# x and the gate loaded in sixteen transfers of falling row counts instead of one of 128 rows

## The chip, the core and the metric

One core of a Trainium2 chip runs the kernel. The metric is the device time of one execution in microseconds; the profile comes from one profiled execution of the same program. TensorE (PE), VectorE (DVE), ScalarE (ACT), GpSimd (POOL) and SyncE (SP) each run their own list of instructions and wait for each other through semaphores; transfers are issued by SP and ACT, each into a queue of its own (q1 and q10 in the profile), and carried out by 16 DMA engines that both queues share.

## The reference

Two sequences of one token, D = 448, 16 heads of 256, a key and value cache of 4096 positions, all in float32.

```python
x = A_x                                                   # (2, 1, 448)
g = sigmoid((x * gate_w).sum(-1, keepdims=True))
q = (x @ wq).reshape(B, 1, 16, 256).transpose(0, 2, 1, 3)
scores = einsum("bhqd,bhkd->bhqk", q, k_cache) * 256 ** -0.5
o = einsum("bhqk,bhkd->bhqd", softmax(scores), v_cache)
a = o.transpose(0, 2, 1, 3).reshape(B, 1, 4096) @ wo
b = maximum(x @ w1, 0) @ w2
return g * a + (1 - g) * b
```

## The kernel before

The cache is read as 32 units, one for each pair of head and sequence. A unit is 128 partitions of 16384 numbers, 64 KB a partition and 8192 KB in all, half keys and half values. There are three buffers for them (`slot`), and every large transfer goes through these: first wq into slot 2 (56 KB a partition), units 0 and 1 into slots 0 and 1, then, in the loop `more` (L126 to L131), each further unit as soon as its slot is free (`free0` to `free2`), and at the end w1 with w2 into slot 2, and wo into slot 0. All of these are issued by SP, in this order, so that two large transfers stand in its queue most of the time.

xg holds x of both sequences and the gate's weights: 128 rows (partitions) of 12 numbers, 48 bytes a row. ACT issues its transfer (L121) as its first instruction, at the same time as SP issues that of wq. The semaphore `xg` counts 16 for a finished transfer. Two engines wait for it: DVE, which spreads x over columns (`xr`, L167, and `xu`, L169), and PE, which multiplies x with the gate (L178, into `pw`) when xr and xu are there.

Behind this on PE stands the query projection: two halves of 16 matmuls each (32 rows in the trace) on wq in slot 2, each with a scaled copy on ACT (`wide`, L184), four transposes (L181) and the placing of the queries in `qt`. When PE has done these it frees slot 2 (`free2`):

```python
    pr.raw(pe, lambda e: (e.sem_inc(sem["room"], 1), e.drain().then_inc(free[2], 1)))
    pr.raw(act, lambda e: pick(e, 0, 0), have_q)
```

That release lets SP issue the load of unit 2 (L131), for which SP has waited since it issued units 0 and 1. ACT picks the first query (L249), and the loop over the units starts: PE makes the scores (L242), DVE their maximum (L261), ACT the exponentials (L254), and DVE eight passes over the values (L265), the last of which frees the unit's slot. PE may start the scores of the next unit after the first of these eight passes (`room`).

After the units come the second branch (w1, w2), the combination of the parts of the softmax, the output projection with wo, and the store.

Of the kernel before, what the change touches and what calls it, by code (L numbers as in the profile page):

```python
# [8 lines left out]
P, HP = 128, 64  # L9
# [58 lines left out]
def gated_mix_decode(nc, xg, kv, wq, w12, wo, out):  # L68
# [22 lines left out]
    def sbuf(name, *shape):  # L91
        return nc.alloc_sbuf_tensor(name, [*shape], F32).ap()
# [9 lines left out]
    sem = {n: nc.alloc_semaphore(n) for n in names}  # L102
    land = [sem[f"land{s}"] for s in range(SLOTS)]
    free = [sem[f"free{s}"] for s in range(SLOTS)]
    pr = Program(nc)
    pe, dve, act, pool, sp = ENGINES
# [9 lines left out]
    def load(s, src, signal, lo=0, hi=None):  # L116
        hi = src.shape[1] if hi is None else hi
        return lambda e: e.dma_start(slot[s][:, lo:hi], src[:, lo:hi]).then_inc(signal, 16)  # L118

    xg_sb = sbuf("xg_sb", P, KC, B + 1)  # L120
    pr.raw(act, lambda e: e.dma_start(xg_sb, xg).then_inc(sem["xg"], 16))  # L121
    pr.raw(sp, load(2, wq, land[2]))
    for u in range(2):
        pr.raw(sp, load(u, kv[u], land[u]))
# [37 lines left out]


    xr = sbuf("xr", P, KC, G, B, RB)
    pr.raw(dve, lambda e: e.wait_ge(sem["xg"], 16))
    for g in range(G):
        pr.op(dve, lambda e, g=g: e.tensor_copy(xr[:, :, g], xg_sb[:, :, :B, None].to_broadcast([P, KC, B, RB])))  # L167
    xu = sbuf("xu", P, KC, UB // B, B)
# [15 lines left out]
        return pr.op(act, lambda e: e.activation(out, src, fn, **kw), *after)  # L184


    pr.raw(pe, lambda e: e.wait_ge(sem["xg"], 16))
    for c in range(KC):
        r = rows_of(c)
        t = mm(pw[0][:, :1], xr[r, c].rearrange("p g b r -> p (g b r)"), xg_sb[r, c, B:], c == 0, c == KC - 1, have_x)  # L190
# [264 lines left out]
```

## Time and profile before

| | us |
|---|---|
| median of 3 runs | 676.48 (676.11 to 676.78) |
| profiled execution | 675.89 |
| its span, first to last instruction | 674.6 |
| busy: DVE, PE, ACT | 341.5, 220.4, 59.7 |
| first DVE copy of x starts | 20.78 |
| load of unit 2 issued | 37.18 |

In the profile a row of the timeline gives start, duration, engine, line, what is written from what, and in brackets how long the engine was idle before it and what ended that. SPq and ACTq are the issues of transfers. A row of the windows gives a stretch, its length, the busy time of PE, its weight load, DVE, ACT and POOL, the granted clock, the share of the DMA engines and the rate; in short windows the last two count a packet's whole size where it starts, so a share can be over 1. In the DMA section a transfer's last number is the time from its issue to its landing, in which all semaphore counts have come.

### The profile page before, as it was taken

To read this page: it belongs to the slowest core of one execution; us is meant where nothing else is said; L and a number is where in the kernel's file an instruction comes from. 1 tells how busy PE (TensorE), PEld (TensorE's weight loads), DVE (VectorE), ACT (ScalarE), POOL (GpSimd) and SP (SyncE) were. 2 spreads that over 40 slices of the span, in tenths; PEclk is the share of its full clock that TensorE was granted. 3 is DMA by queue.
4 is the path that set the end of the run, shared out by engine and by line. 5 is a ranking of instruction groups with operands and counts; after the bars stand their busy time and mean duration, and the time that the engine had idled before them with its cause. 6 is when DMAs were issued, how large, how long until landed. Compare 5 with 4: busy or idle time off the path is not lost. (4 is left out here: it accounts for less than half of the span.)

```text
span 674.6 us, 4162 instructions
## 1 busy us (share of the span) xinstructions
PE 220.4 (33%) x1323; PEld 67.6 (10%) x1323; DVE 341.5 (51%) x571; ACT 59.7 (9%) x121; POOL 0.7 (0%) x6
## 2 busy tenths in 40 slices
PE   0653212333332213333321233333223333331367
PEld 0210000001001000100100010010001001000012
DVE  0006565643655665364566636455564643657661
ACT  0010001001000100100010010001001001000010
POOL 0000000000000000000000000000000000000000
PEclk9976566776656677676556667655666766655789
DMA  9999999999999999999999999999999999999997
GB/s 381 428 435 436 436 435 435 435 435 435 435 435 435 435 435 435 435 435 435 431 435 435 435 435 435 435 435 435 435 435 435 431 435 435 435 435 435 403 424 310
DMA packets 6372, 289.61 MB, mean 429 GB/s; under 512 B 864, under 2 KB 1120, under 8 KB 1632
## 3 DMA queue, kind: packets, MB, share of 16 engines
q1 hardware_dynamic: 6224, 289.55, 99.3%
q8 instruction: 3, 0.05, 0.0%
q10 hardware_dynamic: 144, 0.01, 0.0%
q14 instruction: 1, 0.01, 0.0%
HBM read 289.54 MB, written 0.01 MB: 429 GB/s over the span
## 5 line engine op out<-in xcount | busy, mean ns | idle before, releaser
L265 DVE SCALAR_TENSOR_TENSOR slot<-slot,prob 128x1024 f32<-128x1024 f32 x256 | 295.9, 1221 | 65.3 <-DVEq L65 65.3
L242 PE MATMUL ps<-slot,query 128*32 128x512 f32 x1024 | 186.3, 890 | 406.4 <-PEq L65 406.3
L261 DVE TENSOR_REDUCE nm<-ps 128x1024 f32 (+1 forms) x32 | 39.2, 1224 | 228.8 <-DVEq L65 228.8
L242 PEld LDWEIGHTS ps<-slot,query 128*32 128x32 f32 x1024 | 55.7, 156 | 535.5 <-issue 534.9
L254 ACT ACTIVATE prob<-ps,nm 128x1024 f32<-128x1024 f32 x32 | 35.6, 1113 | 367.2 <-ACTq L65 367.1
L254 ACT ACT_TABLE_LOAD x10 | 12.8, 1283 | 178.7 <-ACTq L65 178.7
L265 DVE DVE_READ_ACCUMULATOR slot<-slot,prob (+1 forms) x256 | 21.2, 83 | 0.0
L178 PE MATMUL pw<-slot,xr 128*32 128x512 f32 (+3 forms) x96 | 13.5, 696 | 1.7 <-PEq L65 1.7
L167 DVE COPY xr<-xg_sb 128x128 f32<-128x128 f32 x4 | 0.6, 220 | 18.5 <-DMA xg_sb<-in_xg 18.5
L178 PE MATMUL pw<-xg_sb,xr 128*128 128x1 f32 (+1 forms) x8 | 1.9, 352 | 21.7 <-DVE xu L169 21.7
L178 PE MATMUL acc<-slot,hr 128*32 128x448 f32 x28 | 6.1, 945 | 2.7 <-DMA slot<-in_w 2.7
L249 ACT ACTIVATE query<-qt 128x2 f32 (+1 forms) x32 | 6.2, 193 | 0.0
L254 ACT ACTIVATION_READ_ACCUMULATOR prob<-ps,nm (+1 forms) x32 | 6.2, 193 | 0.0
L178 PE MATMUL acc<-slot,ot 128*32 128x448 f32 x48 | 5.4, 547 | 1.3 <-DMA slot<-in_wo 1.3
L181 PE MATMUL pw<-ident,nm 128*16 128x128 f32 x2 | 0.7, 330 | 12.6 <-DVEq L315 12.6
L178 PEld LDWEIGHTS pw<-slot,xr 128*32 128x32 f32 (+1 forms) x96 | 2.9, 122 | 10.7 <-issue 10.7
L178 PEld LDWEIGHTS pw<-xg_sb,xr 128*128 128x128 f32 (+1 forms) x8 | 1.8, 320 | 21.6 <-DMA xg_sb<-in_xg 21.6
L181 PE MATMUL pw<-ident,wide 128*128 128x128 f32 x11 | 1.9, 288 | 2.4 <-ACT wide L184 2.4
L383 DVE COPY wide<-acc 128x448 f32<-128x448 f32 x1 | 0.6, 625 | 3.9 <-PE acc L178 3.9
L292 DVE TENSOR_REDUCE nb<-pw 16x1 f32<-16x4 f32 x2 | 0.3, 150 | 4.5 <-PE pw L181 4.5
L178 PE MATMUL pw<-slot,ot 128*32 128x112 f32 x64 | 2.3, 265 | 0.3 <-DMA slot<-in_wo 0.2
L309 DVE COPY ot<-pw 128x256 f32<-128x256 f32 x4 | 1.5, 419 | 1.4 <-PE pw L178 1.4
(42 smaller groups left out, 20.3 us busy)
## 6 DMA issues: line engine op xcount, KB each, us to landing
slot<-in_wq SPq DMA_DIRECT2D x1, 7168.0 KB, 19.8
slot<-in_w SPq DMA_DIRECT2D x2, 3136.0 KB, 30.8
slot<-in_wo SPq DMA_DIRECT2D x2, 1792.0 KB, 20.3
slot<-in_wo SPq DMA_DIRECT2D x3, 896.0 KB, 25.6
slot<-in_kv SPq DMA_DIRECT2D x32, 39.0
slot<-in_wo SPq DMA_DIRECT2D x1, 448.0 KB, 27.9
slot<-in_wo SPq DMA_DIRECT2D x2, 224.0 KB, 28.0
xg_sb<-in_xg ACTq DMA_DIRECT2D x1, 6.0 KB, 20.0
```

Of the source, the lines that this page charges most:

```text
L167: pr.op(dve, lambda e, g=g: e.tensor_copy(xr[:, :, g], xg_sb[:, :, :B, None].to_broadcast([P, KC, B, RB])))
L178: return pr.op(pe, lambda e: e.matmul(out, lhs, rhs, start=start, stop=stop), *after)
L181: return pr.op(pe, lambda e: e.transpose(out, src, ident), *after)
L242: m = e.matmul(ps[g * R:(g + 1) * R, c * CW:(c + 1) * CW], query[s][:, t:t + 1].to_broadcast([P, R]), slot[s][:, lo:lo + CW], start=(t == ...
L249: e.activation(query[s], qt[:, :, bass.ds(u, 1)].rearrange("p t o -> p (t o)"), AF.Copy).then_inc(sem["query"], 1)
L254: e.activation(prob, ps, AF.Exp, bias=nm[:, bass.ds(u, 1)], accum_out=ls[:, bass.ds(u, 1)]).then_inc(sem["prob"], 1)
L261: e.tensor_reduce(nm[:, bass.ds(u, 1)], ps, axis=AX.X, op=ALU.max, negate=True).then_inc(sem["top"], 1)
L265: m = e.scalar_tensor_tensor(v, v, 1.0, prob, op0=ALU.mult, op1=ALU.mult, accum_out=ov[:, bass.ds(u, 1), j])
L292: t = pr.op(dve, lambda e: e.tensor_reduce(nb, mt, axis=AX.X, op=ALU.min), t)
L309: t = pr.op(dve, lambda e, hh=hh: e.tensor_copy(ot[:, i, hh], po[:, hh * B * J:(hh + 1) * B * J].rearrange("p (b j o) -> p j b o", j=J, o= ...
L383: t = pr.op(dve, lambda e: e.tensor_copy(a_sb, acc), t)
```

## The change

The one transfer of 128 rows becomes sixteen, of 15, 14, 13 and so on to 1 rows, and one of 8, issued by ACT one after the other. Each adds 16 to the same semaphore; DVE and PE wait for 256 instead of 16. Bytes, addresses and the rest of the program are the same.

```diff
     xg_sb = sbuf("xg_sb", P, KC, B + 1)
-    pr.raw(act, lambda e: e.dma_start(xg_sb, xg).then_inc(sem["xg"], 16))
+    XG = (*range(15, 0, -1), 8)
+    assert sum(XG) == P
+
+    def load_x(e):
+        lo = 0
+        for k in XG:
+            e.dma_start(xg_sb[lo:lo + k], xg[lo:lo + k]).then_inc(sem["xg"], 16)
+            lo += k
+
+    pr.raw(act, load_x)
...
-    pr.raw(dve, lambda e: e.wait_ge(sem["xg"], 16))
+    pr.raw(dve, lambda e: e.wait_ge(sem["xg"], 16 * len(XG)))
...
-    pr.raw(pe, lambda e: e.wait_ge(sem["xg"], 16))
+    pr.raw(pe, lambda e: e.wait_ge(sem["xg"], 16 * len(XG)))
```

On ACT, at the very start of the program, one issue of 128 rows of 12 numbers stood ahead of the table load and of the gate's activations, which wait for PE:

```order
L60 UNCONDITIONAL_BRANCH [waits barrier_Pool_Activation_PE_DVE_SP_release]
L121 DMA xg_sb<-in_xg 128x12
L184 ACT_TABLE_LOAD
L184 ACTIVATE gp<-pw 128x1 [waits tensor]
L184 ACTIVATE gu<-pw 16x1 [waits tensor]
```

In the changed kernel sixteen stand there (the middle ten are left out here):

```order
L60 UNCONDITIONAL_BRANCH [waits barrier_Pool_Activation_PE_DVE_SP_release]
L128 DMA xg_sb<-in_xg 15x12
L128 DMA xg_sb<-in_xg 14x12
L128 DMA xg_sb<-in_xg 13x12
...
L128 DMA xg_sb<-in_xg 2x12
L128 DMA xg_sb<-in_xg 1x12
L128 DMA xg_sb<-in_xg 8x12
L194 ACT_TABLE_LOAD
L194 ACTIVATE gp<-pw 128x1 [waits tensor]
```

The table load and the first activations of ACT have moved behind fifteen more issues. Nothing moves on the other engines. On SP, the list at the same place shows what the transfers of xg share the DMA engines with, and on which release each load of a unit waits:

```order
L118 DMA slot<-in_wq 128x14336
L118 DMA slot<-in_kv 128x16384 x2
L46 UNCONDITIONAL_BRANCH
L141 ISA [waits free2]
L141 DMA slot<-in_kv 128x16384
L141 ISA [waits free0]
L141 DMA slot<-in_kv 128x16384
```

These rows stand as before, with only the line numbers changed: wq and two units are issued without a wait, unit 2 waits for slot 2, and unit 3 for slot 0.

## The prediction

> **What bounds the kernel now.** I read the shares and the DMA section of the page first, then the start of the timeline, then narrow windows for the DMA engines.
>
> ```profile
> PE 220.4 (33%) x1323; PEld 67.6 (10%) x1323; DVE 341.5 (51%) x571; ACT 59.7 (9%) x121; POOL 0.7 (0%) x6
> DMA  9999999999999999999999999999999999999997
> GB/s 381 428 435 436 436 435 435 435 435 435 435 435 435 435 435 435 435 435 435 431 435 435 435 435 435 435 435 435 435 435 435 431 435 435 435 435 435 403 424 310
> DMA packets 6372, 289.61 MB, mean 429 GB/s; under 512 B 864, under 2 KB 1120, under 8 KB 1632
> q1 hardware_dynamic: 6224, 289.55, 99.3%
> q10 hardware_dynamic: 144, 0.01, 0.0%
> slot<-in_wq SPq DMA_DIRECT2D x1, 7168.0 KB, 19.8
> xg_sb<-in_xg ACTq DMA_DIRECT2D x1, 6.0 KB, 20.0
> out<-res SPq DMA_DIRECT2D x1, 7.0 KB, 1.7
> DMA to landing us min/median/max: 37.0/39.0/57.5
> ```
>
> No compute engine is busy for much over half of the span, while the DMA engines stream at 435 GB/s in nearly every slice. The time is the byte count plus whatever time the stream stands still. So an edit costs only what it adds to the stream, or the time for which it lets the stream run dry. The last row is for the K/V loads: the longest, 57.5 us, is the second one, queued at the start behind wq and the first.
>
> The odd row is xg: 6 KB take 20.0 us to land, as long as the 7168 KB of wq issued at the same moment, while the 7 KB of the output land in 1.7 us once nothing else runs. Hence xg does not travel at its own speed: its pieces wait among wq's.
>
> How big the pieces are: q10 holds 144 packets for xg, which has 128 rows; 16 more are the semaphore writes, one for each of 16 engines. The small packets of the whole program bear this out: 45 transfers times 16 semaphore writes, 128 rows of xg and 16 of the output are 864, the number under 512 B. So each engine has 8 rows of xg and 1 semaphore write, 9 packets, and for wq likewise 8 rows of 56 KB and 1 write. A 56 KB row at 435/16 GB/s takes 2.11 us; a 64 KB row of K/V takes 2.41. The windows show these rows as waves (counted where a packet starts):
>
> ```profile
> 4.60:5.00 0.40, 0.00 (x0) 0.00 (x0) 0.00 (x0) 0.00 (x0) 0.00 (x0) 1.00 4.65 2009
> 5.00:6.60 1.60, 0.00 (x0) 0.00 (x0) 0.00 (x0) 0.00 (x0) 0.00 (x0) 1.00 0.08 36
> 6.60:7.10 0.50, 0.00 (x0) 0.00 (x0) 0.00 (x0) 0.00 (x0) 0.00 (x0) 1.00 3.99 1722
> 57.50:57.80 0.30, 0.00 (x0) 0.00 (x0) 0.30 (x1) 0.00 (x0) 0.00 (x0) 0.50 0.00 0
> 57.80:58.20 0.40, 0.00 (x0) 0.00 (x0) 0.40 (x1) 0.00 (x0) 0.00 (x0) 0.50 2.66 1147
> 58.20:58.60 0.40, 0.00 (x0) 0.00 (x0) 0.40 (x3) 0.00 (x0) 0.00 (x0) 0.50 3.03 1311
> ```
>
> Second rows of wq start at about 4.7, third ones at 6.8. First rows effectively started at 4.7 - 2.11 = 2.6, which is 1.85 after the issue at 0.75. Eight rows of wq end at 2.6 + 16.9 = 19.5, eight of the first K/V at 38.7, eight of the second at 58.0; the wave at 57.8 to 58.6 is the third K/V load following without a gap. If the two queues take turns packet by packet on each engine, xg's 8 rows go between wq's 8 rows and its semaphore write follows wq's: landing just after wq, which is what the rows say (20.0 against 19.8). One xg packet per packet of the big queue is the reading on which all below rests.
>
> Then the work that waits for xg, from the timeline:
>
> ```profile
> 0.75 0.39 ACTq L121 DMA_DIRECT2D xg_sb<-in_xg  x1
> 1.20 0.91 SPq L118 DMA_DIRECT2D slot<-in_kv  x2
> 20.78 0.63 DVE L167 COPY xr<-xg_sb 128x128 f32<-128x128 f32 x4 [18.48 <-DMA xg_sb<-in_xg]
> 21.66 1.92 PE L178 MATMUL pw<-xg_sb,xr 128*128 128x1 f32 x8 [21.66 <-DVE xu L169]
> 23.90 6.34 PE L178 MATMUL pw<-slot,xr 128*32 128x512 f32 x32
> 31.62 3.77 PE L178 MATMUL pw<-slot,xr 128*32 128x512 f32 x32
> 37.17 0.20 ACT L249 ACTIVATE query<-qt 128x2 f32<-128x2 f32 x1
> 37.18 0.35 SPq L131 DMA_DIRECT2D slot<-in_kv  x1
> 40.30 6.56 PE L242 MATMUL ps<-slot,query 128*32 128x512 f32 x32 [3.46 <-PEq L65]
> 59.42 1.22 DVE L265 SCALAR_TENSOR_TENSOR slot<-slot,prob 128x1024 f32<-128x1024 f32 x1
> 59.81 5.35 PE L242 MATMUL ps<-slot,query 128*32 128x512 f32 x32 [12.94 <-PEq L65]
> 60.88 0.34 SPq L131 DMA_DIRECT2D slot<-in_kv  x1
> 79.75 5.62 PE L242 MATMUL ps<-slot,query 128*32 128x512 f32 x32 [14.59 <-PEq L65]
> ```
>
> xg at 20.78 starts the copies of x; both halves of the query projection follow; then PE frees slot 2, and SP issues the third K/V load at 37.18. From xg to that issue: 16.40 us. The queue is full until 58.0, so this issue could come as late as 58.0 - 1.85 = 56.15 and xg as late as 39.75: the cover is 19.0 us.
>
> **The change part by part.** (1) ACT issues 16 transfers instead of 1. At 0.43 us each (SP's first K/V issues take 0.91 for two, with the gap) the last stands at 0.75 + 15 x 0.43 = 7.2 us. ACT's next work, its table load aside, waits for the gate's matmuls, so this costs 0; a dearer issue of 1 us would end at 16 and is covered as well. (2) The bytes are the same; there are up to 112 more semaphore packets. All of xg's 144 packets stay below 0.05% of 16 engines' span in the page, 0.037 us each at most and probably far less: 0.
>
> (3) The pieces no longer divide by 16. Which engines a transfer of 15 rows uses, no row of this profile shows, since every transfer here has 128 or 16 rows. The bounds: dealt out in rotation, each engine gets 8 rows and 8 semaphore writes, 16 turns; dealt from the same first engine each time, one row to an engine, the first engine gets a row and a write of each of the 16 transfers, 32 turns; all rows of an odd transfer on one engine, up to 128 + 16 = 144. What the big queue has for one engine before the third K/V load is 9 + 9 + 9 = 27 packets. The turn that ends the cover is about the 18th, which follows the first K/V load at 38.7 (landing some 0.5 to 1 us later); each further turn costs 2.41 us; from the 27th on it saturates, since the rest of xg goes through an empty queue. So of the interval from 16 to 144 only 16 to 18 is harmless, and all from 27 on comes to the same. I take 32: the split in all 45 transfers is the same for the same shape, which is what a rule by shape alone gives, and a rotation would need a memory of the transfer before.
>
> The Trainium skill has this price: "DMA: Bandwidth & Descriptors", section "Why a DMA increments its semaphore by 16 and not by 1", says that a transfer from such a queue runs on the largest number of engines up to 16 that divides its slowest dimension, and on the lowest-numbered of them; no run here shows it yet. By it the first engine has 32 turns.
>
> (4) xg's last piece then lands just after the second K/V load on that engine. The rows of that load end at 58.0; xg landed 0.5 to 1.3 after its last turn before (19.5 against 20.75, the slowest engine included). So 58.2 to 59.3; I take 58.7. DVE and PE wait there, and everything behind them.
>
> (5) The third K/V load is issued 16.40 later, at 75.1. The projection is the same work on a PE that has idled as before, so I keep its duration. Now the queue is empty. A load into an empty queue: wq's 19.8 us less 16.87 (7168 KB at 435 GB/s) are 2.93 us of start and end; a K/V load of 8192 KB takes 19.28 + 2.93 = 22.2. It lands at 97.3. Before, its scores start at 79.75, and those of the second load 0.6 after its landing (1.66 + 57.5 = 59.2; 59.81): landing at 79.2. Late by 18.1. The bounds: a start as quick as the output's 1.7 in all saves 0.75; xg between 58.2 and 59.3 gives -0.5 to +0.6.
>
> (6) The fourth load needs slot 0, so the first unit's end. Its query is ready 37.37 - 20.78 = 16.6 after xg, at 75.3; scores from 75.6. Before, its scores took 6.56 and from their end (46.86) to the end of its last DVE pass (60.64) 13.8, and SP issued 0.24 later. Scores now: between 3.77 (the second projection half, as many matmuls at a better clock) and 6.56; I take 5.5, as the later units. End 94.9, issue at 95.1 (93.4 to 96.2). To follow without a gap it should be issued by the end of the third load's rows, 75.1 + 1.85 + 19.28 = 96.2, less 1.85: 94.4. Another 0.7 us (0 to 1.8).
>
> (7) After that the slots are ahead again: a backlogged unit takes some 12 us of DVE (rows of the second unit, below, from its reduction to its last pass) against 19.3 of its load, so nothing else is late and nothing is won back, the stream being at its ceiling.
>
> ```profile
> 65.51 1.22 DVE L261 TENSOR_REDUCE nm<-ps 128x1024 f32 x1 [4.87 <-DVEq L65]
> 76.41 1.22 DVE L265 SCALAR_TENSOR_TENSOR slot<-slot,prob 128x1024 f32<-128x1024 f32 x1
> ```
>
> Sum: 18.1 + 0.7 = 18.8 us. The profiled execution took 675.89 (span 674.6), 0.6 below the median of the runs shown; it becomes 694.7, and the median 676.48 becomes 695.3.
>
> **Rivals.** (a) Not slower: the transfers are dealt round the engines, or a row and its semaphore write pass in one turn. Either makes 16 turns on the busiest engine: 9 of wq, 7 rows of the first K/V load, so xg lands at 19.5 + 7 x 2.41 + 1 = 37.4, inside the cover that ends at 39.75, and the time stays 676.5. It decides at 18 turns. Against it: 864 small packets count the semaphore writes as packets of their own; for it, that no row shows the share of an odd transfer.
>
> (b) One engine for all rows of an odd transfer: the 27 turns are used up in the same way and up to 117 packets are left, at most 0.037 each, 4.3 us: 695.3 to 699.6.
>
> (c) The transfers complete one after the other, each at the output's 1.7 us, and do not queue behind big rows: the last at 20.75 + 15 x 1.7 = 46.3, the third K/V issue at 62.7, 6.5 behind 56.15: 683. Against it: the K/V loads issued 0.46 apart follow one another without a gap. The skill's page "DMA: Bandwidth & Descriptors", section "Anatomy of one DMA — SWDGE (gpsimd) path", puts a fixed 2.0 us on each transfer of the other path; taken as serial, that would be an estimate of 687. No run here shows it.
>
> (d) Faster: nothing in the stream gets shorter; only noise.
>
> **How the numbers follow.** My forecast 0.87, (a) 0.06 with its threshold case, (b) 0.04, (c) 0.02, (d) 0.01. The time is that of the likeliest, 695.3. Its own range, from the bounds in (4) to (6), is 693 to 698. The range for 8 in 10 reaches a little lower, to 691, for a quicker start of an empty queue and a better clock together, and up to 699 for most of (b). A difference under 0.2% (1.35 us; the three runs lie within 0.1%) counts as none: faster 0.01, same 0.05, slower 0.94.
>
> **What the profile after would show.** q10 with about 256 packets (128 rows, and 15 + 14 + ... + 1 + 8 = 128 writes); the first copy of x on DVE near 58.7; the third K/V issue near 75.1; a hole in the GB/s row in the fourth and fifth slice (50.6 to 84.3) worth 18 us, and full slices after it. If q10 has its packets but the copy starts near 37, (a) is right; near 46, (c). If the copy starts at 58.7 and the time is not up by 17 to 20, the empty queue's start or the fourth load's wait is mis-sized.

## Result and the profile after

| | before | changed |
|---|---|---|
| median, us | 676.3 (675.94 to 676.78) | 695.9 (695.79 to 695.93) |
| profiled execution, span, us | 675.89, 674.6 | 695.92, 694.6 |
| first DVE copy of x, us | 20.78 | 59.60 |
| load of unit 2 issued, us | 37.18 | 76.03 |

The ratio is 1.0292 (95% interval 1.0280 to 1.0305): 19.6 us slower, where 18.8 had been forecast (695.3). The two profiled executions differ by 20.0 us in their spans, since the one before lay 0.4 us under its median.

The page after, its DMA rows and the two queues:

```profile
DMA  9992599999999999999999999999999999999997
GB/s 387 459 423 121 242 423 457 438 430 423 426 426 460 438 423 426 423 442 453 430 423 426 426 464 434 423 426 423 460 442 423 426 423 453 442 430 426 419 424 315
q1 hardware_dynamic: 6224, 289.55, 96.6%
q10 hardware_dynamic: 256, 0.01, 0.0%
```

The stream has one hole, in the fourth and fifth slice (52 to 87 us); in every other slice the engines are as busy as before, though the rate now swings between 419 and 464 GB/s where it stood at 435. q10 has 256 packets: 128 rows and 128 semaphore writes, which is one write for each engine that a transfer uses, with as many engines as rows.

These rows of the timeline after show the chain that made the hole:

```profile
0.75 6.46 ACTq L128 DMA_DIRECT2D xg_sb<-in_xg  x16
7.24 1.28 ACT L194 ACT_TABLE_LOAD   x1 [7.24 <-issue]
59.60 0.63 DVE L177 COPY xr<-xg_sb 128x128 f32<-128x128 f32 x4 [57.30 <-DMA xg_sb<-in_xg]
60.49 1.92 PE L188 MATMUL pw<-xg_sb,xr 128*128 128x1 f32 x8 [60.49 <-DVE xu L179]
62.73 6.35 PE L188 MATMUL pw<-slot,xr 128*32 128x512 f32 x32
70.47 3.77 PE L188 MATMUL pw<-slot,xr 128*32 128x512 f32 x32
76.03 0.35 SPq L141 DMA_DIRECT2D slot<-in_kv  x1
76.53 3.64 PE L252 MATMUL ps<-slot,query 128*32 128x512 f32 x32 [0.83 <-PEq L65]
94.16 0.34 SPq L141 DMA_DIRECT2D slot<-in_kv  x1
99.66 6.58 PE L252 MATMUL ps<-slot,query 128*32 128x512 f32 x32 [7.05 <-PEq L65]
```

The sixteen issues are over at 7.2 us, yet DVE waits until 59.60. The projection then runs as before, and SP can issue the load of unit 2 at 76.03 only. In windows of the changed kernel (the last two numbers are the DMA share and GB/s) the engines start their last rows of unit 1 just after 55.5 (1049 GB/s over 1 us is 16 rows of 64 KB) and then nothing but a few small packets until that load arrives:

```profile
55.50:56.50 1.00, 0.00 (x0) 0.00 (x0) 0.00 (x0) 0.00 (x0) 0.00 (x0) 1.00 2.42 1049
56.50:57.90 1.40, 0.00 (x0) 0.00 (x0) 0.00 (x0) 0.00 (x0) 0.00 (x0) 1.00 0.00 0
57.90:58.70 0.80, 0.00 (x0) 0.00 (x0) 0.00 (x0) 0.00 (x0) 0.00 (x0) 1.00 0.02 0
58.70:76.90 18.20, 13.98 (x92) 5.22 (x96) 0.89 (x6) 2.25 (x9) 0.00 (x0) 1.00 0.00 0
76.90:78.00 1.10, 1.10 (x16) 0.46 (x12) 0.00 (x0) 0.00 (x0) 0.00 (x0) 1.00 2.78 953
```

Before, the wave at 57.8 to 58.6 followed here without a gap. The row with 0.00 over 18.2 us is nearly the whole loss. The share of 0.02 at 57.9 to 58.7 holds the last xg packets, passing with unit 1's semaphore writes at the end of its load, where the forecast put them.

### The profile page after: what moved, and what is told of

It reads as the page before. It is cut to its first block, busy times and chain, and to the rows that moved or that the text cites. A ratio compares the mean times of both kernels' runs of the same rounds, so it can differ in the third digit from the quotient of the medians.

```text
span 694.6 us, 4177 instructions
## 1 busy us (share of the span) xinstructions
PE 211.6 (30%) x1323; PEld 64.6 (9%) x1323; DVE 341.4 (49%) x571; ACT 59.8 (9%) x121; POOL 0.7 (0%) x6
## 5 line engine op out<-in xcount | busy, mean ns | idle before, releaser
L252 PE MATMUL ps<-slot,query 128*32 128x512 f32 x1024 | 178.5, 856 | 396.5 <-PEq L65 396.4
L252 PEld LDWEIGHTS ps<-slot,query 128*32 128x32 f32 x1024 | 52.9, 150 | 520.7 <-issue 520.2
```

Source lines behind the costliest of these rows:

```text
L252: m = e.matmul(ps[g * R:(g + 1) * R, c * CW:(c + 1) * CW], query[s][:, t:t + 1].to_broadcast([P, R]), slot[s][:, lo:lo + CW], start=(t == ...
```

## Experiments

The theory to be tested: the two queues take turns packet by packet on each engine, a semaphore write is a turn of its own, the engine with the most xg packets decides, and a delay is free while the big queue still has work (the cover). The rivals: what counts is the number of transfers, each at a fixed price; the uneven shares, or the sixteen transfers themselves, are slow; every microsecond of xg's delay costs one.

**Two transfers only.**

```diff
-    XG = (*range(15, 0, -1), 8)
+    XG = (127, 1)
```

> Two transfers only, of 127 rows and of 1. Turns theory (the queues alternate packet by packet on each engine, and the engine with the most xg packets decides): 127 has no divisor up to 16 but 1, so all rows go to one engine, 130 packets against the 27 of the big queue; xg lands after the second unit's load as with sixteen transfers, plus about 100 packets through an empty queue at the 0.013 us seen between two of them, 1.3 us. First DVE copy near 60.5, time about 697 (696 to 700); q10 shows 130 packets. Count theory (each further transfer costs a turn of 2.42 us, whatever its rows): first copy near 23, time 676.3.

Measured: 694.91 us, ratio 1.0273 (1.0256 to 1.0290). The queue of xg on this kernel's page:

```profile
q10 hardware_dynamic: 130, 0.01, 0.0%
```

And its timeline, the copy of x and the issue for unit 2:

```profile
59.47 0.63 DVE L177 COPY xr<-xg_sb 128x128 f32<-128x128 f32 x4 [57.16 <-DMA xg_sb<-in_xg]
75.09 0.35 SPq L141 DMA_DIRECT2D slot<-in_kv  x1
```

Two transfers cost as much as sixteen, so the number of transfers is not the price. The 130 packets are 128 rows and only one semaphore write for each transfer: each ran on one engine. The copy came 1 us earlier than expected, and the time of 694.91 lies just below the expected 696 to 700. The packet records of the trace (start, length, size and queue of every DMA packet) say why: 55 of the rows had passed by 2.6 us, before wq's first row held that engine, and the 50 packets left after unit 1 followed one another in 0.007 us each, so they cost almost nothing.

**Eight transfers of 16 rows.**

```diff
+    XG = (16,) * 8
```

> Eight transfers of 16 rows, one row on each engine from each: 8 rows and 8 semaphore writes an engine. Turns theory with a semaphore write as a turn of its own: 16 turns, after 9 packets of wq and 7 rows of the first unit: first DVE copy near 37 to 38, inside the cover, time 676.3 as before. Turns theory with the write passing together with its row: 8 turns, first copy near 20.8. Both give no change of time; the copy's start tells them apart. q10 256 packets in both.

Measured: 676.23 us, ratio 1.0002 (0.9993 to 1.0012). Page, timeline and windows of this kernel, in this order:

```profile
q10 hardware_dynamic: 256, 0.01, 0.0%
```

```profile
37.23 0.63 DVE L177 COPY xr<-xg_sb 128x128 f32<-128x128 f32 x4 [34.93 <-DMA xg_sb<-in_xg]
52.76 0.35 SPq L141 DMA_DIRECT2D slot<-in_kv  x1
```

```profile
56.40:58.00 1.60, 0.49 (x8) 0.00 (x0) 0.77 (x1) 0.00 (x0) 0.00 (x0) 1.00 0.00 0
58.00:58.70 0.70, 0.00 (x0) 0.00 (x0) 0.45 (x1) 0.05 (x1) 0.00 (x0) 1.00 3.47 1498
```

The same 256 packets in the queue, but 16 on each engine instead of 32 on the first: the copy starts at 37.23, so each semaphore write does take a turn (8 turns would have given 20.8). xg is 16.5 us later than before and it costs nothing: unit 2's rows follow at 58.0 with no gap beyond the wave's own pause (1.6 us here, as between the waves of the kernel before). That is the cover.

**Twenty, twenty-two and eighteen turns.** Transfers of 16 rows give every engine one row and one write, transfers of 8 give them to eight engines alone, so the turns of the busiest engine can be dialled, two for each transfer.

```diff
+    XG = (16,) * 6 + (8,) * 4
...
+    XG = (16,) * 5 + (8,) * 6
...
+    XG = (16,) * 7 + (8,) * 2
```

> Six transfers of 16 rows and four of 8: engines 0 to 7 get 10 rows and 10 writes, 20 turns; the others 12. Turns theory: the last follows the second row of the second unit (43.6 to 44.3), first DVE copy near 44.5 to 45, 4.8 us past the end of the cover at 39.75: third K/V issue near 61.1, time about 681 (680 to 682). Count theory: 20.78 plus nine times 2.42 is 42.6, time 679. If the big queue were not the cover at all but each us of xg's delay cost a us: 676.3 + 24 = 700.

> Five transfers of 16 rows and six of 8: 22 turns on engines 0 to 7. Turns theory: one row and one write more than with 20 turns, so two rows of the second unit later: first DVE copy near 44.40 + 4.83 = 49.2, third K/V issue 64.5 to 65.6, time 685.2 to 686.2. If a semaphore write took no turn of its own: copy near 46.8, time near 683.

> Seven transfers of 16 rows and two of 8: 18 turns on engines 0 to 7, the edge of the cover. Turns theory: the last row follows unit 0's last row and the last write unit 0's semaphore write, near 39.0: first DVE copy near 39.7, third K/V issue 55 to 56.2, time 676.3 to 676.7, no loss to be measured. If the cover were shorter than the 19.0 us worked out, up to 2 us slower.

| turns | first copy | load of unit 2 issued | median, us | ratio (95% interval) |
|---|---|---|---|---|
| 16 | 37.23 | 52.76 | 676.23 | 1.0002 (0.9993 to 1.0012) |
| 18 | 39.85 | 55.28 | 677.33 | 1.0014 (1.0004 to 1.0023) |
| 20 | 44.40 | 59.64 | 680.38 | 1.0063 (1.0046 to 1.0080) |
| 22 | 49.36 | 64.94 | 684.98 | 1.0131 (1.0110 to 1.0152) |

The timelines, of 20, of 22 and of 18 turns in this order:

```profile
44.40 0.63 DVE L177 COPY xr<-xg_sb 128x128 f32<-128x128 f32 x4 [42.09 <-DMA xg_sb<-in_xg]
59.64 0.35 SPq L141 DMA_DIRECT2D slot<-in_kv  x1
```

```profile
49.36 0.63 DVE L177 COPY xr<-xg_sb 128x128 f32<-128x128 f32 x4 [47.06 <-DMA xg_sb<-in_xg]
64.94 0.35 SPq L141 DMA_DIRECT2D slot<-in_kv  x1
```

```profile
39.85 0.63 DVE L177 COPY xr<-xg_sb 128x128 f32<-128x128 f32 x4 [37.55 <-DMA xg_sb<-in_xg]
55.28 0.35 SPq L141 DMA_DIRECT2D slot<-in_kv  x1
```

From 20 to 22 turns the copy moves by 4.96 us, two rows of a unit (4.83), and the time by 4.6. From 16 to 18 it moves by 2.62: of the two added turns one follows unit 0's semaphore write and not a row. The count of transfers does not fit: for the ten transfers of 20 turns it gave a copy at 42.6 and 679 us, against 44.40 and 680.38.

The time starts to rise near where the cover was worked out to end: copies 4.6 and 9.6 us past 39.75 cost 4.1 and 8.8 us. (With 20 turns the load came 1.5 us before the expected 61.1, since the first half of the projection took 5.18 us and not 6.34.) With 18 turns the load is issued at 55.28, before the 56.15 that was the latest harmless moment. The 1.1 us measured are within what was set as no difference, but 677.33 lies above the expected 676.3 to 676.7 and the interval leaves out 1. The packet records show a part of it: unit 2's first rows start without a gap at 58.05 to 58.59, but they take 2.42 to 3.56 us where all of them took 2.42 with 16 turns. That is 0.28 us on average, and this execution's span is 0.4 us longer than before, so the cover seems to end somewhat before the 56.15 that was worked out. The rest of the 1.1 us stays open.

**The same sixteen transfers in the big queue.**

```diff
-    pr.raw(act, load_x)
     pr.raw(sp, load(2, wq, land[2]))
+    pr.raw(sp, load_x)
```

> The sixteen transfers of the changed kernel, but issued by SP in the big queue between wq and unit 0, so there are no turns between two queues on any engine. Turns theory: the small packets follow wq's rows in order and pass at about 0.013 us each, their semaphore writes landing some 0.17 us apart: first DVE copy near 21 to 23, inside the cover; SP's sixteen issues (about 7 us) end at 8.1, before wq's rows do at 19.5: time 676.3 to 677. If sixteen transfers or their uneven shares cost the time by themselves (issue, completion one after the other, the first engine's load): still 690 to 696.

Measured: 676.8 us, ratio 1.0010 (1.0000 to 1.0020). The timeline of this kernel, then its windows:

```profile
1.20 5.92 SPq L128 DMA_DIRECT2D xg_sb<-in_xg  x16
23.19 0.63 DVE L177 COPY xr<-xg_sb 128x128 f32<-128x128 f32 x4 [20.89 <-DMA xg_sb<-in_xg]
39.95 0.35 SPq L141 DMA_DIRECT2D slot<-in_kv  x1
```

```profile
19.00:20.20 1.20, 0.00 (x0) 0.00 (x0) 0.00 (x0) 0.00 (x0) 0.00 (x0) 1.00 2.83 879
21.50:22.60 1.10, 0.00 (x0) 0.00 (x0) 0.00 (x0) 0.00 (x0) 0.00 (x0) 1.00 1.10 477
22.60:23.20 0.60, 0.00 (x0) 0.00 (x0) 0.01 (x1) 0.00 (x0) 0.00 (x0) 1.00 0.00 0
23.20:24.90 1.70, 0.82 (x4) 0.85 (x5) 0.73 (x5) 0.00 (x0) 0.00 (x0) 1.00 1.42 617
```

The transfers, their shares and their 256 semaphore counts are those of the changed kernel; the turns between two queues are gone, and with them the loss. (SP now issues them, so units 0 and 1 are issued at 7.2 instead of 1.2, long before wq's rows end.) The windows show a small rest. All sixteen engines start unit 0 in the window from 19.00, as they should after wq: 879 GB/s over 1.2 us is 16 rows of 64 KB and the 6 KB of xg. Their second rows are due 2.4 us later, but only eight start in the window from 21.50 (477 GB/s over 1.1 us), and the others after 23.2. In the packet records the first rows of those others took 3.5 to 4.5 us instead of 2.42.

**Even shares on eight engines.**

```diff
+    XG = (8,) * 16
```

> Sixteen transfers of 8 rows: engines 0 to 7 get 16 rows and 16 writes, 32 turns, the other eight none. Turns theory: as with the falling row counts, first DVE copy near 59.5, third K/V issue 75 to 76, time 695 to 696. If what cost the time were the one overloaded engine (sharply uneven shares), eight engines sharing would land it earlier: copy well before 59.

Measured: 695.36 us, ratio 1.0289 (1.0272 to 1.0307). In its timeline:

```profile
59.65 0.63 DVE L177 COPY xr<-xg_sb 128x128 f32<-128x128 f32 x4 [57.35 <-DMA xg_sb<-in_xg]
74.85 0.35 SPq L141 DMA_DIRECT2D slot<-in_kv  x1
```

Eight engines with 32 turns land xg when one engine with 32 does. It also shows that transfers of 8 rows start at the same engines each time: with the starts in rotation this kernel would have had 16 turns, and a copy near 37.

**The sixteen transfers alone.**

```diff
+    pr.raw(sp, lambda e: e.wait_ge(sem["xg"], 16 * len(XG)))
     pr.raw(sp, load(2, wq, land[2]))
```

> The sixteen transfers of the changed kernel, with wq and all behind it issued only when xg has landed, so that xg has the engines to itself. Turns theory: xg lands about 1.3 us after its last issue at 6.9, first DVE copy near 8.5, wq issued near 8.5 instead of 0.75, time 676.3 + 7.8 = 684. If the sixteen transfers were slow by themselves (each 1.7 us, one after the other): copy near 28, time near 704.

Measured: 683.07 us, ratio 1.0099 (1.0082 to 1.0116). In its timeline:

```profile
7.72 0.63 DVE L178 COPY xr<-xg_sb 128x128 f32<-128x128 f32 x4 [5.42 <-DMA xg_sb<-in_xg]
7.72 0.39 SPq L118 DMA_DIRECT2D slot<-in_wq  x1
```

With the engines to themselves the sixteen transfers have landed by 7.72, 1.0 us after the end of their last issue (6.70), and 0.8 before the expected 8.5. Had they gone one after the other, it would have been near 28. wq starts 6.97 us later than before, and the time is 6.85 us longer. So the transfers are not slow by themselves. They are held up.

No variant beat the kernel before, and none was expected to: an xg that arrives earlier only lengthens a cover that is already long enough.

## Why the prediction was right, point by point

- **The bound.** Right: bytes over 435 GB/s plus the hole. Of the 20.0 us by which the span grew, 18.2 are one window without traffic.
- **One xg packet per packet of the big queue, semaphore writes included.** Shown, by 16, 20 and 22 turns landing where their turns put them, and by the loss vanishing when both stand in one queue. The packet records of the changed kernel show it directly: 15 rows of xg pass at 4.54 to 5.24 us, their 15 semaphore writes at 6.67 to 7.36, the 14 rows of the next transfer at 8.79 to 9.48, each one row of wq (2.12 us) after the last.
- **Step 3, the split.** As forecast: as many engines as rows, from the same first one. The 256 packets give the first half, sixteen transfers of 8 rows the second, and two transfers of 127 and 1 the case of one engine. The Trainium skill's rule in "DMA: Bandwidth & Descriptors", section "Why a DMA increments its semaphore by 16 and not by 1" (the largest divisor up to 16, on the lowest-numbered engines) agrees with the 256 and the 130 packets; which numbers the engines bear, these rows do not say.
- **Step 3, saturation.** Shown: 32 and 130 turns give copies at 59.60 and 59.47.
- **Step 1, ACT's issues at no cost.** The last ended at 7.2, as said, and the table load moved from 1.17 to 7.24, long before 62, where ACT is next wanted.
- **Step 4, xg's landing, mis-sized by 0.9.** 59.60 for 58.7, just outside its bounds of 58.2 to 59.3. The last packets of xg did pass by 58.55, but ten semaphore writes pass there together and land one after another, from 58.64 to 59.58, so the last took 1.0 us where before one took about 0.5 (19.44 to 19.96).
- **Step 5, the load into an empty queue, mis-sized by 1.0.** The projection took 16.43 again (76.03 less 59.60). The load took 23.2 and not 22.2:

```profile
DMA to landing us min/median/max: 23.2/38.6/57.5
```

  (The row is that of the K/V loads; its least value is the load of unit 2, the only one issued into an empty queue.) One row of that load came late. Narrow windows of the changed kernel show a wave of 64 KB rows, a pause, and a single row:

```profile
82.40:83.10 0.70, 0.00 (x0) 0.00 (x0) 0.00 (x0) 0.70 (x1) 0.00 (x0) 1.00 3.33 1428
83.10:83.70 0.60, 0.00 (x0) 0.00 (x0) 0.00 (x0) 0.59 (x2) 0.00 (x0) 1.00 0.00 0
83.70:84.00 0.30, 0.00 (x0) 0.00 (x0) 0.00 (x0) 0.30 (x1) 0.00 (x0) 1.00 0.60 218
```

```profile
q8 instruction: 3, 0.05, 0.0%
```

  The wave of 1428 GB/s over 0.7 us is 15 rows and 16 KB more. The packet records name these 16 KB: a packet of the queue q8, which the page lists as `instruction` with three packets. It starts at 82.89, where the sixteenth engine's next row was due, and takes 0.96 us; that row starts at 83.84. Fifteen engines' semaphore writes land by 97.92, which is 21.9 us after the issue, and the last one at 99.22. So the forecast's 22.2 was close for a load without this packet. The kernel of twenty turns bears it out: its first q8 packet comes at 85.9, after the load of unit 2, and that load took 21.9. With 22 turns the packet falls into the load (78.8), and the last engine landed 1.2 us behind the others. The kernel before has such a packet as well, at 62.99, but there it left the last engine only 0.4 us behind. What the packet holds is not shown.
- **Step 6, the fourth load, 0.7 too much.** The scores of the first unit took 3.64 and not 5.5, at a granted clock of 1.00 (the window from 76.90); before, they took 6.56 at a mean of 0.55. So its slot was free and the load issued at 94.16, before 94.4 and well before the 95.3 that this bound becomes when unit 2 is issued at 76.03 instead of 75.1. Even the lower bound of 3.77 was a little long. What kept the clock up is not shown.
- **The sum.** 18.1 + 0.9 + 1.0 and nothing for step 6 is 20.0, the span's 674.6 to 694.6. The scores of unit 2 moved by 99.66 - 79.75 = 19.91, so all of it was lost by then and nothing came back, as step 7 said. The three errors, of 1 us or less each, cancelled in part, and that they did is luck.

## What to carry to other kernels

A transfer's size tells little of when it lands if it shares engines with a large stream: count its packets on its busiest engine, semaphore writes included, and take a full row of the stream for each. Make the row count of a transfer a multiple of 16, so that no engine carries more of it than another, and put a small load that others wait for into the same queue at the place where it is wanted, where it pays no turns (676.8 us here instead of 695.9). And find the cover first: a delay of 16.5 us was free, and what went past the 19.0 us of cover cost nearly its full length.

## What the runs showed of the hardware that was not expected

- The first half of the query projection, the same 32 rows, took 5.13 to 6.67 us at a granted clock of 1.00, the second 3.77 each time. The shortest, from the timeline of sixteen transfers of 8 rows, and the longest, from that of the transfers behind wq:

```profile
62.77 5.13 PE L188 MATMUL pw<-slot,xr 128*32 128x512 f32 x32
```

```profile
26.33 6.67 PE L188 MATMUL pw<-slot,xr 128*32 128x512 f32 x32
```

  That is why the kernel of sixteen transfers of 8 issued unit 2's load 15.2 us after its copy, and the changed kernel 16.4 after its own. What sets the spread stays open.
- A run of small packets with semaphore writes is not free for the engine that carries it: behind wq, eight engines started unit 0's second row about 1.6 us after the others (the windows from 21.50 and from 23.20). The small packets themselves pass quickly, a row with its write every 0.013 us in the packet records, which makes 0.2 us for sixteen of them. It is the 64 KB row behind them that grows. Each engine's count can be matched by its times (wq's last row ends, the small packets pass, unit 0 starts): behind up to four rows of xg with their writes it takes 2.42 us, behind nine 3.53, and behind sixteen 4.45. That kernel's 0.5 us (ratio 1.0010) would fit, but it was not measured by itself.
- The queue that the page lists as `q8 instruction` brings three packets of 16 KB in a run. The one in the load of unit 2 takes a turn of 0.96 us on one data engine, and the load lands later for it: by 1.3 us in the changed kernel, and by 1.4 with sixteen transfers of 8 rows (fifteen engines by 96.57, the last at 97.95).
